# Order of the loads and of the score tiles around batch 1's attention, in a fused forgetting attention and GELU MLP

## The chip, the cores and the metric

The kernel runs on one core of one Trainium2 chip. A core has five engines that run at the same time, each through its own queue of instructions in order: TensorE (PE, matrix products; its weight loads are listed as PEld), VectorE (DVE), ScalarE (ACT, which has the exp and the GELU), GpSimd (POOL) and SyncE (SP, which only issues DMAs). Sixteen DMA engines move data between HBM and SBUF; their work comes from queues, and here the loads that POOL issues go through queue 0 and those that SP issues through queue 1. Matmuls write to PSUM, which has eight banks per partition. The metric is the device time of one execution in microseconds; the trace of one profiled execution says where it went.

## What is computed

```python
def _attn_ref(q, k, v, f):                  # q, k, v: (8, 8, 576, 64)   f: (8, 8, 576)
    scores = np.matmul(q, k.transpose(0, 1, 3, 2)) / np.sqrt(D)
    cum = np.cumsum(np.log(np.clip(f, 0.0001, 1.0)), axis=-1)
    decay = cum[:, :, :, None] - cum[:, :, None, :]
    scores = np.where(causal, -1000000000.0, scores + decay)
    attn = softmax(scores)                  # written out in the source
    return np.matmul(attn, v)

def _moe_ref(x, w_in, w_out):               # (4608, 512), (512, 2048), (2048, 512)
    h = x @ w_in
    g = 0.5 * h * (1.0 + erf(h / sqrt(2)))
    return g @ w_out

x = attn_out.transpose(0, 2, 1, 3).reshape(B * S, H * D)
```

There are 8 batches of 8 heads, 576 tokens and 64 features, then an MLP over the 4608 rows that the attention gives.

## The kernel before

**Tiles.** A batch is worked through in four pairs of heads (i = 0 to 3). For a pair, q and k have to stand transposed in `qT[i]` and `kT[i]`, features on the partitions, the two heads in the two halves. The causal triangle of scores of a pair is cut into four tiles (t = 0 to 3, `STILES` at L30): each is computed by PE into one of two score buffers of two PSUM banks (`scores`, L299), turned into `e` by one exp on ACT (L309), and, where it crosses the diagonal, masked. Batch 0 and pair 0 of batch 1 are masked by extra matmuls on PE; all others by POOL (L311), five instructions for a pair: two on tile 0, one on each of the others. Both score buffers are taken in turn, so a tile's matmuls wait until the exp of the tile two before it is done.

**v.** The forget gate enters as weights on v: `weigh_v(b, i)` multiplies the two heads of pair i by their weights (L268) and writes the weights in an extra column (L275). It runs on POOL for batch 1 and later. `attend` (L330) then multiplies e by the weighed v, 15 matmuls for a head, into one of two PSUM banks of the pool `o_psum`; `normalize` on DVE divides by the sums (L343, L344) and writes x. x is transposed into `xT`, by PE and a copy in batches 0 and 1 (`to_xT`, L363 and L366), by a DMA in the later ones (`x_dma`, L369).

**The MLP.** `gemm1` (L385) multiplies xT of a batch by w_in, one block of 128 features at a time, and ACT takes the GELU (L405). The second GEMM is spread as filler among the next attention's score tiles, through generators that `take(fill, n)` moves on by n matmuls. For batch 1 the filler is the first half of batch 0's rows, `gemm2_half(0, 0)` at L517: two PSUM banks, 16 matmuls, the first eight with the first quarter of w_out, the others with the second quarter. Batches 2 and later have longer fillers (L479).

**The order** is written out by hand: the context is `manual_schedule`, and each engine runs its instructions as the program lists them. `first_attention` holds batch 0, `second_attention` batch 1, `attention(b)` the rest. Between attentions the main loop at L727 runs the remaining blocks of `gemm1` and hangs preparation for the next batch on some of them.

**Loads.** POOL issues q, k, w_in and w_out (with a cast to bf16, L107, L171, L175). Each issue occupies POOL for 0.7 to 0.8 us. SP issues v in five pieces for the five blocks of 128 keys (`load_v`, L119, into the single buffer `v_sb`), the transposing DMAs of q and k of batch 2 and later (`transpose_dma`, L235) and of x, and the stores (L497). A queue of instructions is in order: an instruction that waits holds what is behind it. There is a small device for ordering a load behind something else: a one-column instruction on POOL that reads or writes a tile, so that what follows has to wait. The `memset` of a column of `v_sb` is one (the load of v that follows writes there, so it waits for POOL), `gate` another.

In batch 0's attention POOL issues, in this order, w_in's four quarters, q and k of batch 1 in two halves of four heads; SP issues v of batch 1 in two halves, one after the other. POOL then weighs pair 0 of batch 1 (program place: block 12 of the main loop for batch 0), issues w_out's quarters 0 and 1, weighs pair 1, and issues q and k of batch 2. The third and fourth quarters of w_out follow after the last score tile of batch 1. In `second_attention` each score tile is followed by something else: transposes of the next pair's q and k in pair 0, two filler matmuls in pairs 2 and 3, one head of the pair before after tiles 1 and 2.

`transposes_first` transposes q or k of a pair on PE (L207), six blocks of each head: first those of one head, then those of the other; the two heads go to the two halves of the PSUM partitions.

Of the kernel before, what the change touches and what calls it, by code (L numbers as in the profile page):

```python
# [8 lines left out]
FP32 = mybir.dt.float32  # L9
# [5 lines left out]
P = 128  # L15
S = 576
D = 64
H = 8
HP = 4
# [4 lines left out]
JT = 6  # L24
PT = 96
# [27 lines left out]
def kernel(  # L53
# [60 lines left out]
    def load_v(b, h0=0, h1=H):  # L114
        if b >= B:
            return
        for n in range(NBLK):
            p0 = D if n == NBLK - 1 else 0
            nc.sync.dma_start(  # L119
                v_sb[p0:P, h0:h1, n, :],  # L120
                v[b, h0:h1, K0[n] + p0 : K0[n] + P].rearrange("h p d -> p h d"),
            )
# [78 lines left out]
    def transposes_first(b, i, which, pool, tag):  # L201

        src = qk_of[b][which]
        ps = pool.tile([P, JT, PT], BF16, tag=tag, name="ps_f")
        for h in range(2):
            for j in range(JT):
                nc.tensor.transpose(  # L207
                    ps[h * D : (h + 1) * D, j, :],
                    src[:, 2 * i + h, j * D : (j + 1) * D],
                    ident_bf[:PT, :PT],  # L210
                )

        dst = (qT, kT)[which][i].rearrange("d (p j) -> d p j", j=JT)
        src = ps.rearrange("d j p -> d p j")
        if b or i:
            nc.vector.tensor_copy(dst, src)
        elif which:
            nc.vector.tensor_copy(dst[:, 0 : PT // 2], src[:, 0 : PT // 2])
            nc.scalar.copy(dst[:, PT // 2 :], src[:, PT // 2 :])
        else:  # L220
            nc.scalar.copy(dst, src)
# [315 lines left out]
    def take(gen, n):  # L537
        for _ in range(n):
            if next(gen, "end") == "end":
                return  # L540


    def gate(h, n):

        t = x_pool.tile([P, 1], FP32, tag="gate", name="gate")
        nc.gpsimd.tensor_copy(t[D:P], v_sb[D:P, h, n, 0:1])

    def first_attention():


# [44 lines left out]
        load_w_in(2)  # L595
        nc.gpsimd.memset(v_sb[:, :, 0, 0:1], 0.0)
        load_v(1, 0, 4)
        load_v(1, 4, 8)
        load_w_in(3)
        load_qk_tokens(1, 0, 4)  # L600
        load_qk_tokens(1, 4, 8)
        scores(0, 2, 1)
        heads = [(i, h) for i in range(3) for h in range(2)]
        for i, t in ((2, 2), (2, 3), (3, 0), (3, 1), (3, 2), (3, 3)):
# [28 lines left out]

    FILL = [[7, 6, 3, 3], [1, 3, 3, 2], [1, 3, 3, 3], [1, 3, 3, 3], [5]]
    FILL_2 = [[8, 8, 8, 8], [8, 8, 4, 4], [4, 4, 4, 4], [4, 4, 4, 4], [4]]
    FILL_1 = [[0, 0, 0, 0], [0, 0, 0, 0], [2, 2, 2, 2], [2, 2, 2, 2]]

    def attention(b):

# [9 lines left out]
        for i in range(HP):  # L649
            for t in range(4):  # L650
                scores(b, i, t)
                take(fill, counts[i][t])
                if i and t == 1:
                    av(i - 1)
                    x_dma(b, i - 1)
                if b == 2 and (i, t) == (0, 3):
                    weigh_v(b, 2)
                    weigh_v(b, 3)
                if i == 0 and t == (3 if b == 2 else 1):
                    load_v(b + 1)  # L660
                if b > 2 and t == 0 and i < 2:
                    transpose_dma(b + 1, 4 * i, 4 * i + 4)
                if b == 2 and t == 1 and i == 1:
                    transpose_dma(3, 0, 4)
# [21 lines left out]
    def second_attention():  # L686


        b, fill = 1, gemm2_half(0, 0)

        def av(i, h):
            attend(b, i, h, (0, 1, 2, 3, 4))
            normalize(b, i, h)

        def transposes(i, pool, tag):
            for which in range(2):
                transposes_first(b, i, which, pool, tag)


        nc.scalar.activation(warm[0:1, 0:1], warm[0:1, 0:1], Act.Exp)  # L700
        for i in range(HP):
            for t in range(4):
                scores(b, i, t)
                if i == 0 and t < 3:
                    transposes(t + 1, *((m_psum, "m") if t == 1 else (o_psum, "o")))
                take(fill, FILL_1[i][t])
                if i and t in (1, 2):
                    av(i - 1, t - 1)
                if i > 1 and t == 0:
                    to_xT(b, i - 2, nc.vector.tensor_copy, o_psum, "o")  # L710
                if i == 1 and t % 2:
                    weigh_v(1, 2 + t // 2)
                if (i, t) == (3, 3):
                    load_w_out(2)
                    load_w_out(3)
                if (i, t) == (3, 0):
                    transpose_dma(2, 0, 4)
                    transpose_dma(2, 4, 8)
        to_xT(b, HP - 2, nc.vector.tensor_copy, o_psum, "o")
        av(HP - 1, 0)  # L720
        av(HP - 1, 1)
        both = s_psum.tile([P, 2, 1024], BF16, tag="s", name="ps_x2")
        gemm1_begin(1, both)
        x_tail(1)
        load_v(2)

    for b in range(B):  # L727
# [8 lines left out]
        for ffb in range(4 if b < 2 else 5, n_ff):  # L736
            gemm1(b, ffb, ps=spare() if b > 1 and ffb in (7, 8) else None)
            if b == 0:
                if ffb == 14:
                    for which in range(2):  # L740
                        transposes_first(1, 0, which, o_psum, "o")
                if ffb == 12:
                    weigh_v(1, 0)
                    load_w_out(0)
                    load_w_out(1)
                    weigh_v(1, 1)
                    load_qk_tokens(2)
# [43 lines left out]
```

## Time and profile before

| | us |
|---|---|
| five runs | 342.55, 342.9, 343.3, 343.54, 343.72 |
| their median | 343.3 |
| the profiled execution, all of it | 344.4 |
| its span, from the first to the last instruction of the program | 342.3 |
| PE busy in the span | 327.4 |
| ACT / DVE / POOL busy | 209.7 / 185.1 / 121.7 |
| attention of batch 0, to the first GEMM | 0 to about 25 |
| first GEMM of batch 0 | 25 to 39.16 |
| attention of batch 1 | 39.16 to 60.45 |
| first GEMM of batch 1 | 60.45 to 73.59 |
| attention of batch 2 | 73.59 to 105.64 |

A span is counted from the first to the last instruction; the time of an execution has about 2 us around it. "Busy" is the time in which an engine runs at least one instruction. Matmuls are pipelined, so their listed durations overlap. In a timeline, a row gives the start, the busy time, the engine, the line, the operation, output and input tiles, the shape and, in brackets, how long the engine was idle before it and what ended that. In the chain of waits each row is the start, the length and the piece of work that was waited for. In the rows of the DMA queues the numbers are packets, MB, and the time that the packets took as a share of the sixteen engines.

The stretch that the change rewrites ends 60 us into the program; after it the same 280 us of GEMMs and attentions follow.

### The profile page before, as it was taken

How to read it: one execution, taken by the hardware profiler on the slowest of the kernel's cores; microseconds unless marked ns; L12 is line 12 of the kernel's file. 1: busy time of each engine (PE TensorE's matmuls, PEld its weight loads, DVE VectorE, ACT ScalarE, POOL GpSimd, SP SyncE). 2: the span in 40 equal slices, each digit the busy share in tenths (PEclk: the TensorE clock that was granted, in tenths of full speed). 3: DMA queues.
4: the chain of work that ended last, by engine and by line, in shares of the span. 5: the costliest groups of instructions: out<-in, count | busy, mean ns of one | idle time of the engine just before them, and what ended most of it. 6: DMA issues, size and time to landing. Idle time of an engine off the chain costs nothing.

```text
span 342.3 us, 7789 instructions
## 1 busy us (share of the span) xinstructions
PE 327.4 (96%) x3130; PEld 172.9 (51%) x3170; DVE 185.1 (54%) x418; ACT 209.7 (61%) x298; POOL 121.7 (36%) x247
## 2 busy tenths in 40 slices
PE   8799979999999999999999999999999999999995
PEld 4574545444554456545644465445544554444443
DVE  4770445662556944796469646984597541020011
ACT  6976777584553687378737873787468755504600
POOL 8190196009346134533445242724351420000000
PEclk9999999999999999999999999999999999999999
DMA  8999989997998989496977698589910242011013
GB/s 118 177 146 188 193 135 186 160 184 146 213 191 193 138 160 206 116 137 87 209 184 108 110 212 159 92 139 194 186 38 2 61 93 50 0 62 63 0 37 86
DMA packets 104627, 44.16 MB, mean 129 GB/s; under 512 B 83408, under 2 KB 100048, under 8 KB 104592
## 3 DMA queue, kind: packets, MB, share of 16 engines
q1 hardware_dynamic: 87296, 29.52, 44.5%
q0 software_dynamic: 16896, 13.63, 26.9%
q8 instruction: 24, 0.39, 0.5%
q10 hardware_dynamic: 400, 0.52, 0.4%
q14 instruction: 11, 0.09, 0.1%
HBM read 36.85 MB, written 9.44 MB: 135 GB/s over the span
## 4 chain that ended last, share of the span: by engine, by line
PE 82%; SPq 6%; DMA 4%; POOL 3%; issue 2%; DVE 1%; ACT 0%; POOLq 0%; DVEq 0%; ACTq 0%
PE ps L385 32%; PE ps L479 26%; PE o L330 8%; PE ps L421 8%; SPq L119 6%; PE s L299 6%; PE ps L517 2%; DMA v_sb<-in_v_dram 2%; DMA w_out_sb<-in_moe_w_out_dram 2%; POOL vw L268 1%; POOL q L107 1%; POOL k L107 0%; DVE vw L268 0%; DVE x L344 0%; PE ps_x L363 0%
## 5 line engine op out<-in xcount | busy, mean ns | idle before, releaser
L405 ACT ACTIVATE g<-ps 128x512 bf16<-128x512 f32 x144 | 82.1, 602 | 81.8 <-PE ps L385 81.8
L309 ACT ACTIVATE e<-s 128x896 bf16<-128x896 f32 (+2 forms) x128 | 101.4, 835 | 30.1 <-PE s L299 26.9
L385 PE MATMUL ps<-xT,w_in_sb 128*128 128x512 bf16 x502 | 111.7, 379 | 0.5
L479 PE MATMUL ps<-w_out_sb,g 64*128 64x512 bf16 (+1 forms) x712 | 102.1, 376 | 0.9 <-issue 0.5
L385 PEld LDWEIGHTS <-w_in_sb 128*128 128x128 bf16 x576 | 56.0, 98 | 67.5 <-issue 1.8
L311 POOL TENSOR_SCALAR_AFFINE_SELECT e<-e 128x256 bf16<-128x256 bf16 (+1 forms) x135 | 49.1, 383 | 94.9 <-ACT e L309 94.6
L479 PEld LDWEIGHTS <-g 64*128 64x128 bf16 (+1 forms) x736 | 41.9, 94 | 40.2 <-issue 9.3
L268 POOL TENSOR_TENSOR vw<-v_sb,wT 128x640 bf16<-128x640 f32 x30 | 38.6, 1289 | 38.3 <-DMA v_sb<-in_v_dram 30.0
L299 PE MATMUL s<-qT,kT 64*128 64x320 bf16 (+4 forms) x384 | 45.9, 277 | 2.8 <-ACT e L309 2.4
L249 DVE COPY kT<-tk 64x288 bf16<-64x288 bf16 x96 | 42.7, 445 | 3.3 <-DMA tk<-k 1.8
L249 DVE COPY qT<-tq 64x288 bf16<-64x288 bf16 x96 | 40.3, 420 | 3.0 <-DMA tq<-q 1.6
L330 PE MATMUL o<-vw,e 128*128 128x65 bf16 x960 | 37.1, 194 | 3.6 <-issue 2.4
L487 DVE COPY ot<-ps 128x512 f32<-128x512 f32 x25 | 17.3, 692 | 41.8 <-PE ps L479 41.8
L330 PEld LDWEIGHTS <-e 128*128 128x128 bf16 x960 | 34.5, 98 | 8.2 <-POOL e L311 2.8
L344 DVE TENSOR_TENSOR x<-o,r 128x320 bf16<-128x320 f32 x64 | 31.5, 492 | 2.2
L430 DVE COPY ot<-ps 128x512 f32<-128x512 f32 (+2 forms) x9 | 5.7, 633 | 48.8 <-PE ps L421 46.1
L299 PEld LDWEIGHTS <-kT 64*128 64x128 bf16 x384 | 19.3, 94 | 22.7 <-issue 9.4
L421 PE MATMUL ps<-w_out_sb,g 128*128 128x512 bf16 (+2 forms) x142 | 27.9, 355 | 0.1
L343 DVE RECIPROCAL r<-o 128x5 f32<-128x5 f32 x64 | 12.2, 190 | 22.5 <-PE o L330 22.5
L421 PEld LDWEIGHTS <-g 128*128 128x128 bf16 x144 | 13.5, 98 | 14.5
L490 DVE TENSOR_TENSOR ot<-ot,ps 128x512 f32<-128x512 f32 x25 | 17.2, 688 | 1.7 <-PE o L330 0.5
L385 PE MATMUL ps<-tails,w_in_sb 128*128 128x512 bf16 x62 | 14.2, 378 | 0.2
(64 smaller groups left out, 137.9 us busy)
## 6 DMA issues: line engine op xcount, KB each, us to landing
out_dram<-ot SPq DMA_DIRECT2D x32, 256.0 KB, 2.6
v_sb<-in_v_dram SPq DMA_DIRECT2D x24, 256.0 KB, 5.0
q<-in_q_dram POOLq DMA_DIRECT2D x6, 576.0 KB, 6.3
k<-in_k_dram POOLq DMA_DIRECT2D x6, 576.0 KB, 8.4
v_sb<-in_v_dram SPq DMA_DIRECT2D x22, 128.0 KB, 5.8
w_in_sb<-in_moe_w_in_dram POOLq DMA_DIRECT2D x4, 512.0 KB, 8.0
w_out_sb<-in_moe_w_out_dram POOLq DMA_DIRECT2D x4, 512.0 KB, 8.0
q<-in_q_dram POOLq DMA_DIRECT2D x4, 144.0 KB, 4.7
```

What stands on the lines that cost most here:

```text
L119: nc.sync.dma_start(v_sb[p0:P, h0:h1, n, :], v[b, h0:h1, K0[n] + p0 : K0[n] + P].rearrange("h p d -> p h d"),)
L249: nc.vector.tensor_copy(rows[:, odd], src[odd * D : (odd + 1) * D, 2 * i + h].rearrange("d j p -> d p j"),)
L268: eng.tensor_tensor(vw(b)[:, hs, :, 0:D], v_sb[:, hs, :, :], w.unsqueeze(3).to_broadcast([P, 2, NBLK, D]), Alu.mult,)
L299: nc.tensor.matmul(to, *ab, start=half < 0, stop=half == 1 or not masked)
L309: nc.scalar.activation(et[:, :, z:c], st[:, :, z:c], Act.Exp, scale=scale)
L311: nc.gpsimd.affine_select(out=et[:, :, c0 + z : c0 + P], in_=et[:, :, c0 + z : c0 + P], compare_op=Alu.is_ge, fill=0.0, base=z, pattern=[[ ...
L330: nc.tensor.matmul(o[:, m, :], e_of[b, i, t][:, h, c : c + P], vw_of[b][:, 2 * i + h, n, :], start=(n == 0), stop=(n == m),)
L344: nc.vector.tensor_tensor(x_of[b, i][:, :, h, :], o[:, :, 0:D], r.unsqueeze(2).to_broadcast([P, NBLK, D]), Alu.mult,)
L385: nc.tensor.matmul(ps, w_in_sb[:, kt, ffb * P : (ffb + 1) * P], src[:, kt, 0:TC], start=(kt == 0), stop=(kt == n_dm - 1),)
L405: nc.scalar.activation(g_of[c][ffb], ps, Act.Gelu)
L421: nc.tensor.matmul(pss[ts][:, c0:c1], g_of[c][kt][:, ts * P : (ts + 1) * P], w_out_sb[:, kt, c0:c1], start=(kt == 0), stop=(kt == n_ff - 1),)
L479: nc.tensor.matmul(banks[r], g_of[c][kt][rows, ts * P : (ts + 1) * P], w_out_sb[rows, kt, :], start=kt == (steps.index("r") if r else 0), ...
```

## The change

Four things change.

- In `first_attention`, `load_v(1, 4, 8)` is taken out and `load_w_out(0)` is put behind the loads of q and k of batch 1. At block 12 of the main loop for batch 0, `behind(qk_of[1][0], H - 1)` makes POOL wait until q's second half has landed, a `memset` of `v_sb`'s heads 4 to 7 makes SP wait for that, and `load_v(1, 4, 8)` follows; `load_w_out(0)` is no longer there.
- `second_attention` is written out anew: score tiles come two at a time (`tiles`), the transposes of pairs 1 and 2 stand behind the first two tiles and those of pair 3 behind the next two, both heads of a pair are attended together (`run`), the 16 filler matmuls come in four groups of four, and the transposes of x of pairs 0, 1 and 2 come later than before. The transposes of x of pair 2 go to a score buffer, and their copy to ACT in place of DVE. A second `behind` makes POOL wait for k of batch 2 before it issues w_out's third and fourth quarters.
- In `attention(2)`, `load_v(3)` is moved from behind tile 3 of pair 0 to behind the transposing DMA of x of pair 0.
- `transposes_first` alternates between the two heads instead of doing one after the other, in batches 0 and 1.

```diff
--- before.py
+++ after.py
@@ -202,8 +202,8 @@
-        for h in range(2):
-            for j in range(JT):
+        for j in range(JT):
+            for h in range(2):
                 nc.tensor.transpose(
                     ps[h * D : (h + 1) * D, j, :],
                     src[:, 2 * i + h, j * D : (j + 1) * D],
@@ -545,6 +545,11 @@
+    def behind(t, h):
+
+        g = x_pool.tile([P, 1], FP32, tag="gate", name="gate")
+        nc.gpsimd.tensor_copy(g[:PT], t[:, h, 0:1])
+
     def first_attention():
@@ -595,10 +600,10 @@
         load_w_in(2)
         nc.gpsimd.memset(v_sb[:, :, 0, 0:1], 0.0)
         load_v(1, 0, 4)
-        load_v(1, 4, 8)
         load_w_in(3)
         load_qk_tokens(1, 0, 4)
         load_qk_tokens(1, 4, 8)
+        load_w_out(0)
         scores(0, 2, 1)
@@ -633,7 +638,6 @@
-    FILL_1 = [[0, 0, 0, 0], [0, 0, 0, 0], [2, 2, 2, 2], [2, 2, 2, 2]]
@@ -653,10 +657,12 @@
                 if i and t == 1:
                     av(i - 1)
                     x_dma(b, i - 1)
+                    if b == 2 and i == 1:
+                        load_v(3)
                 if b == 2 and (i, t) == (0, 3):
                     weigh_v(b, 2)
                     weigh_v(b, 3)
-                if i == 0 and t == (3 if b == 2 else 1):
+                if b > 2 and i == 0 and t == 1:
                     load_v(b + 1)
@@ -698,28 +704,45 @@
-        for i in range(HP):
-            for t in range(4):
-                scores(b, i, t)
-                if i == 0 and t < 3:
-                    transposes(t + 1, *((m_psum, "m") if t == 1 else (o_psum, "o")))
-                take(fill, FILL_1[i][t])
-                if i and t in (1, 2):
-                    av(i - 1, t - 1)
-                if i > 1 and t == 0:
-                    to_xT(b, i - 2, nc.vector.tensor_copy, o_psum, "o")
-                if i == 1 and t % 2:
-                    weigh_v(1, 2 + t // 2)
-                if (i, t) == (3, 3):
-                    load_w_out(2)
-                    load_w_out(3)
-                if (i, t) == (3, 0):
-                    transpose_dma(2, 0, 4)
-                    transpose_dma(2, 4, 8)
-        to_xT(b, HP - 2, nc.vector.tensor_copy, o_psum, "o")
-        av(HP - 1, 0)
-        av(HP - 1, 1)
+        def tiles(i, t):
+            scores(b, i, t)
+            scores(b, i, t + 1)
+
+        def run(i):
+            av(i, 0)
+            av(i, 1)
+
+        tiles(0, 0)
+        transposes(1, o_psum, "o")
+        transposes(2, m_psum, "m")
+        tiles(0, 2)
+        transposes(3, m_psum, "m")
+        tiles(1, 0)
+        run(0)
+        tiles(1, 2)
+        take(fill, 4)
+        weigh_v(1, 2)
+        tiles(2, 0)
+        run(1)
+        weigh_v(1, 3)
+        tiles(2, 2)
+        take(fill, 4)
+        tiles(3, 0)
+        transpose_dma(2, 0, 4)
+        transpose_dma(2, 4, 8)
+        take(fill, 4)
+        to_xT(b, 0, nc.vector.tensor_copy, o_psum, "o")
+        tiles(3, 2)
+        behind(qk_of[2][1], H - 1)
+        load_w_out(2)
+        load_w_out(3)
+        run(2)
+        to_xT(b, 1, nc.vector.tensor_copy, o_psum, "o")
+        take(fill, 4)
+        av(3, 0)
         both = s_psum.tile([P, 2, 1024], BF16, tag="s", name="ps_x2")
+        to_xT(b, 2, nc.scalar.copy, ps=both[:, 0, 0:XC])
+        av(3, 1)
         gemm1_begin(1, both)
         x_tail(1)
         load_v(2)
@@ -740,8 +763,10 @@
                 if ffb == 12:
+                    behind(qk_of[1][0], H - 1)
+                    nc.gpsimd.memset(v_sb[:, 4:8, 0, 0:1], 0.0)
+                    load_v(1, 4, 8)
                     weigh_v(1, 0)
-                    load_w_out(0)
                     load_w_out(1)
                     weigh_v(1, 1)
                     load_qk_tokens(2)
```

## The prediction

> **What bounds the kernel now.** I read the busy shares first, then the stretch that the change rewrites (batch 1's attention) by windows, then the chain of waits through it, then POOL's and the DMA queues' part of that chain.
>
> ```profile
> PE 327.4 (96%) x3130; PEld 172.9 (51%) x3170; DVE 185.1 (54%) x418; ACT 209.7 (61%) x298; POOL 121.7 (36%) x247
> ```
>
> TensorE (PE) is busy for 96% of the span, so a change gains only where PE stands idle. Batch 1's attention runs from 39.16 us, when batch 0's first GEMM has been issued, to 60.45, where the last x of batch 1 is transposed and batch 1's first GEMM streams.
>
> ```profile
> 39.16:44.50 5.34, 4.23 (x106) 3.33 (x107) 4.22 (x7) 5.13 (x8) 3.20 (x5) 1.00 0.66 134
> 44.50:49.45 4.95, 3.16 (x48) 2.03 (x49) 1.46 (x5) 3.81 (x5) 4.95 (x9) 1.00 0.99 154
> 49.45:57.46 8.01, 7.93 (x100) 4.36 (x99) 4.33 (x11) 5.54 (x7) 5.44 (x15) 1.00 1.30 200
> 57.46:60.45 2.99, 2.68 (x43) 1.88 (x45) 1.77 (x5) 2.00 (x3) 1.92 (x3) 1.00 1.10 153
> 60.45:73.59 13.14, 13.09 (x62) 5.74 (x60) 9.19 (x28) 8.63 (x15) 0.42 (x1) 1.00 1.18 184
> ```
>
> The columns after the stretch and its length are busy us of PE, weight load, DVE, ACT, POOL, then clock, DMA share, GB/s. PE idles 1.1 us in the first stretch and 1.8 in the second, where POOL is busy throughout; from 49.45 it is packed, and after 60.45 too. The clock is full, so none of this is throttling. What the second stretch waits for stands in the chain:
>
> ```profile
> 37.22 4.02 DMA v_sb<-in_v_dram
> 41.30 1.27 POOL vw L268
> 42.67 5.94 DMA w_out_sb<-in_moe_w_out_dram
> 48.65 0.38 PE ps L517
> 57.77 0.41 POOL e L311
> 60.16 0.45 PE ps_x L363 x5
> ```
>
> The first quarter of w_out is issued by POOL only after POOL has waited for v and weighed a pair; it lands 5.94 us later, and PE, which has the matmul at L517 next, starts it at 48.65 after 1.44 us of waiting. Batch 1's remaining score tiles stand behind it, so ACT starves too. At the end a mask of POOL (57.77) decides.
>
> **The change, part by part.** *w_out(0) earlier.* It joins POOL's queue behind batch 1's q and k, and is in SBUF some 4 us earlier, so the 1.44 us go. What is late next is POOL:
>
> ```profile
> 41.30 1.27 POOL L268 TENSOR_TENSOR vw<-v_sb,wT 128x640 bf16<-128x640 f32 x1 [14.98 <-DMA v_sb<-in_v_dram]
> 42.67 1.56 POOL L175 DMA_DIRECT2D w_out_sb<-in_moe_w_out_dram  x2
> 45.60 0.84 POOL L107 DMA_DIRECT2D q<-in_q_dram  x1
> 47.20 1.02 POOL L311 TENSOR_SCALAR_AFFINE_SELECT e<-e 128x256 bf16<-128x256 bf16 x3
> ```
>
> Let W be the start of the first weighing. POOL then has that weighing with its small copy, 1.37 (41.30 to 42.67); one w_out issue, 0.78 (half of 1.56); the second weighing, 1.37; q and k of batch 2, 1.60 (45.60 to 47.20); and pair 1's five masks, 1.71 (three from 47.20 to 48.18, two from 49.55 to 50.29). Pair 1 is masked at W+6.83. W cannot come before 41.3, since v's first half keeps its place in its queue; it can come up to 1 us later, because w_out's packets now take engines that v had alone near the end (below). I take 41.6, near the first bound, as the slowest engines were still carrying k then. Masks done: 48.45.
>
> PE's new order needs that mask in head (1,0): ten of its 15 matmuls and head (1,1) follow, 0.8 us by the row at 58.23 (25 matmuls in 0.97): 49.3. Then two score tiles 0.55; four L517 matmuls, 0.86 (eight took 1.73); tile (3,0); a wait of 0.3, as tile (3,1) needs the exp of (2,3) to free its buffer, and exps run at 0.6 to 0.8 each; 51.7. Four L517, 0.86; transposes of x(0), 0.35; tiles (3,2), (3,3) 0.6, to 53.5. Pair 2's two heads 1.0, to 54.5. Transposes of x(1) need the PSUM bank of head (2,0), free when DVE's reciprocal and multiply end (0.39 to start, 0.2 + 0.5): a wait of 0.6, to 55.1, and 0.3 of work. Four L517 to 56.3; head (3,0) 0.55; transposes of x(2) 0.4; head (3,1) 0.5 and drain: 58.0. In the trace of before, 1.25 us lie between that point (58.23 + 0.97 = 59.20) and 60.45. So 59.25 in place of 60.45: **1.2 us earlier**. ACT is covered: its sixteen exps need 11.6 us from 41.2 (five took 3.62), and the last mask, after exp (3,3) at about 54.9, is done by 55.4, before head (3,0) at 56.3 asks. Without that cover each us of lateness costs one.
>
> *Half of v later.* Heads 4 to 7 of batch 1 are issued once POOL has seen q land (23.76 + 15.2 = 38.96): about 39.2. They are 4x128 + 64 KB in 256 B packets, 2304 of them.
>
> ```profile
> q0 software_dynamic: 2087, 1.75, 91.3%
> q1 hardware_dynamic: 2034, 0.51, 32.1%
> ...
> q1 hardware_dynamic: 993, 0.25, 112.7%
> q0 software_dynamic: 28, 0.02, 11.1%
> ```
>
> The first two lines are 26 to 38 us: beside a full queue 0 (POOL's) v gets one packet for one, 170 per us. The last two are 40 to 41 us: alone it gets 993 per us. w_out(0) is 512 packets of 1 KB; with queue 0 at 667 in 4 us (22 to 26 us) it ends near 43. Queue 0 is then empty until w_out(1), issued at W+1.37 = 43.0, sends its first packet, about 1.9 us later (in the trace of before none has moved by 44, issued at 42.67). So v has the engines alone for nearly 2 us, 1900 packets, and a rest of up to 400 at 170 per us. It lands between 45.5 and 49. Call it L. Pair 2's heads come at L + 1.37 + 0.98 + 1.37 + 0.73 = L + 4.45 (two weighings, four steps of masks; POOL is in order, so masks of pair 2 queue behind the weighing that waits). They are due at 53.5: L up to 49.05 is free, and from 50.25 on the change loses.
>
> The Trainium skill, "DMA: Bandwidth & Descriptors", section Specifications, gives about 0.6 us to the first byte for a DMA issued by SP. This trace differs: of v issued at 21.81, 32 packets had moved by 26, against 667 of queue 0. By the page v would start at 39.8 and land early in my interval, by the row late in it; the sum is 342.1 by either.
>
> *w_out(1), batch 2's q and k.* Their issues on POOL are counted above. w_out(1) is asked for by the third group of L517 at 51.7 and lands by 43.0 + 5.94 = 48.9; cover 2.8 us. k of batch 2 follows about 3 us earlier than its 57.8 (46.42 + 11.4), as one w_out quarter less stands ahead of it. The gate on k ahead of w_out(2), (3) therefore opens near POOL's last mask, and the transposes and v of batch 2, which hang on k in SP's queue, move forward as much or more than PE. Cost 0; were k no earlier, w_out(2) would land at 65.4 as now (58.12 + 7.3), still ahead of 72.7, when the first matmul of batch 2's fill reads it (73.89 - 1.2).
>
> *Transposes with heads alternating.* In the trace 24 of them take
>
> ```profile
> 39.91 0.47 PE L207 MATMUL ps_f<-key_of,q 96*64 96x96 bf16 x10
> ...
> 40.66 0.20 PE L299 MATMUL s<-qT,kT 64*128 64x64 bf16 x2
> ```
>
> 0.75 us, 31 ns each. Gain between 0 and 0.1 us per group, off the path: the groups of batch 0 end in the wait for v, those of batch 1 in ACT's table load, which ends at 41.1. The Trainium skill, "TensorEngine Tiling (Array Packing)", section Theoretical Speedup, promises up to 2x for 64 columns, which would be 0.37 per group; the rows around 40.2, where q's and k's transposes start in turns, show that most of the overlap is there already. The price is 0 by both, as the groups lie under other waits.
>
> *x of batch 2 ahead of v(3).* SP issues the transposing DMA of x (93.90 in the trace) before v's five, which take 7.67 us of SP from 85.38. x is 6 us earlier, nobody waits for it before 105.6; v lands perhaps 2 us later than its 95.8 (90.46 + 5.3), read at 101.47 by a POOL instruction that then waits for PE anyway. Price 0, with 0.5 either way if these covers are thinner than they look.
>
> **Sum.** The profiled execution has a span of 342.3 us, 344.4 in all; 2.1 lie around the span. 342.3 - 1.2 = 341.1. The five runs have a median of 343.3, 1.1 below the profiled one, so I put the gain on the median: **342.1 us**. The likeliest case's own range is 340.6 (W at 41.3, neither wait of PE: 2.4 gained, and 0.3 of the spread of the runs) to 343.0.
>
> **Rivals.** (a) *The wait only moves to POOL, nothing is left:* with W at 42.6, as w_out's packets hold up the end of v's first half, every step above shifts by 1 us and 59.25 becomes 60.25: 343.1. For it: POOL is busy for all of the second stretch. Against it: the slowest engines had no free time to lose. (b) *v's second half comes late:* if queue 0 never runs dry, L = 40.7 + 2304/170 = 54.3, pair 2 starts at 58.75 in place of 53.5, and GEMM at 64.5: 4 us lost, 347.3; it loses from L = 50.25. For it: the one-for-one share over 12 us. Against it: POOL cannot issue w_out(1) before it has weighed a pair. (c) *Given back later:* the GEMM starts 1.2 us earlier but batch 2's loads do not; PE then waits at 71 to 85 and the time is 343.3. Against it: k and v of batch 2 move with it.
>
> **How the numbers follow.** Of a difference under 0.2% (0.7 us) a measurement of this kernel cannot tell. The forecast has 0.60; (a) and (c) 0.17 together; (b) 0.23, most of it with L between 51 and 54, 344 to 347. Faster 0.60, same 0.17, slower 0.23. The range that leaves out 2 in 10 reaches from 340.5 to 345.0.
>
> **What would show it.** Right: no wait for w_out at L517; POOL's first weighing at 41.3 to 42; the weighing of pair 2 at POOL without a wait for v, or one ending by 49; GEMM streaming at 59.25, and the same 281.9 us from there to the end. Wrong: POOL waiting for v past 50; PE waiting on a mask or on DVE between 49 and 56 for more than 0.9 us in all; a first weighing after 42.5; or new idle time of PE after 60.

## The result and the profile after

Side by side the changed kernel takes 341.7 us (median of 54 runs, 340.61 to 347.39) and the kernel before 343.71 (94 runs, 342.15 to 347.54). The ratio is 0.9948, with a 95% interval of 0.9936 to 0.9959: 1.4 to 2.2 us faster. The forecast was 342.1. In 12 of the 54 executions the mean granted clock of PE was below 0.998, and these have a median of 344.15; the other 42 have 341.3. The profiled execution took 341.23, with a span of 339.2.

The busy shares of the changed kernel, from its page:

```profile
PE 325.6 (96%) x3129; PEld 171.6 (51%) x3170; DVE 184.4 (54%) x417; ACT 209.9 (62%) x299; POOL 121.8 (36%) x250
```

No engine has less work to speak of (PE's 1.8 us are within what such a total moves: two traces of the kernel before have 327.4 and 331.8, the first with 40 matmul records fewer). What changed is how long the stretch of batch 1's attention takes. Its windows, with the same columns as before (stretch and length, busy us of PE, weight load, DVE, ACT, POOL, then clock, DMA share, GB/s):

```profile
38.50:43.50 5.00, 3.84 (x110) 3.00 (x110) 3.55 (x6) 4.91 (x8) 3.90 (x6) 1.00 1.13 208
43.50:48.50 5.00, 4.75 (x80) 2.99 (x79) 2.69 (x8) 4.46 (x6) 4.28 (x8) 1.00 1.23 191
48.50:54.35 5.85, 5.26 (x63) 3.08 (x64) 2.93 (x8) 4.65 (x7) 5.29 (x16) 1.00 1.23 182
54.35:57.35 3.00, 2.95 (x47) 2.01 (x46) 1.72 (x5) 2.11 (x3) 1.51 (x2) 1.00 1.19 101
57.35:70.50 13.15, 13.04 (x62) 5.79 (x62) 10.26 (x32) 9.08 (x16) 0.42 (x1) 1.00 1.21 203
```

In what follows "the section" runs from the first score tile of batch 1 (39.45 before, 38.50 after) to the GEMM behind the last transposes of x (60.45 and 57.35). It falls from 21.01 to 18.86 us. After it come 281.89 us before and 281.85 after, the same. The remaining 0.95 us of the difference between these two spans lies ahead of the section; a second trace of the kernel before has its first tile at 38.94, so part of that is the spread from execution to execution.

The clearest view of the section is ScalarE's timeline (start, busy time, operation, tiles, shape of the first, count; in brackets the idle time before the row and what ended it). The kernel before:

```profile
41.21 2.40 ACT L309 ACTIVATE e<-s 128x896 bf16<-128x896 f32 x3
43.77 3.62 ACT L309 ACTIVATE e<-s 128x640 bf16<-128x640 f32 x5 [0.16 <-PE s L299]
47.62 0.92 ACT L309 ACTIVATE e<-s 128x896 bf16<-128x896 f32 x1 [0.23 <-ACT e L309]
49.89 0.81 ACT L309 ACTIVATE e<-s 128x768 bf16<-128x768 f32 x1 [1.36 <-PE s L299]
...
56.99 0.70 ACT L309 ACTIVATE e<-s 128x640 bf16<-128x640 f32 x1 [0.34 <-PE s L299]
```

The changed kernel:

```profile
40.26 4.68 ACT L309 ACTIVATE e<-s 128x896 bf16<-128x896 f32 x6
45.10 1.51 ACT L309 ACTIVATE e<-s 128x896 bf16<-128x896 f32 x2 [0.17 <-PE s L299]
46.98 3.03 ACT L309 ACTIVATE e<-s 128x896 bf16<-128x896 f32 x4 [0.37 <-ACT e L309]
50.33 3.24 ACT L309 ACTIVATE e<-s 128x896 bf16<-128x896 f32 x4 [0.32 <-PE s L299]
```

Sixteen exps, one for each score tile. Before, they stretch over 16.49 us (41.21 to 57.70), with 3.77 us of gaps, the largest (1.36) where PE stood at L517 for w_out and could not feed ACT. After, they are packed into 13.31 us (40.26 to 53.57) with 1.02 us of gaps. So each section is a sum of three pieces: 1.76 us from the first score tile to the first exp, the stretch of exps, and a tail from the last exp to the GEMM.

| | first exp | stretch of exps | tail | section |
|---|---|---|---|---|
| before | 1.76 | 16.49 | 2.75 | 21.01 |
| changed | 1.76 | 13.31 | 3.78 | 18.86 |

The exps gain 3.18 us, and the tail gives 1.03 back: the new order leaves pair 2's heads, a group of filler and two groups of x transposes behind the last score tile. The difference is 2.15 us.

POOL's timeline in the changed kernel answers to the rows shown of before:

```profile
39.59 1.27 POOL L268 TENSOR_TENSOR vw<-v_sb,wT 128x640 bf16<-128x640 f32 x1 [1.49 <-DMA v_sb<-in_v_dram]
...
40.95 0.81 POOL L175 DMA_DIRECT2D w_out_sb<-in_moe_w_out_dram  x1
...
43.98 0.78 POOL L107 DMA_DIRECT2D k<-in_k_dram  x1
44.76 1.01 POOL L311 TENSOR_SCALAR_AFFINE_SELECT e<-e 128x256 bf16<-128x256 bf16 x3
46.09 0.41 POOL L311 TENSOR_SCALAR_AFFINE_SELECT e<-e 128x256 bf16<-128x256 bf16 x1 [0.31 <-ACT e L309]
46.68 0.41 POOL L311 TENSOR_SCALAR_AFFINE_SELECT e<-e 128x256 bf16<-128x256 bf16 x1 [0.19 <-ACT e L309]
47.30 1.28 POOL L268 TENSOR_TENSOR vw<-v_sb,wT 128x640 bf16<-128x640 f32 x1 [0.22 <-POOL e L311]
...
54.06 0.18 POOL L551 CAST gate<-k 96x1 f32<-96x1 bf16 x1
```

The first weighing starts at 39.59; pair 1 is masked at 47.09 (46.68 + 0.41); the last two of these masks wait for ACT, not ACT for them. The weighing of pair 2 follows 0.2 us later. And PE's timeline, the three rows on which the prediction had put a number:

```profile
45.23 1.04 PE L517 MATMUL ps<-w_out_sb,g 128*128 128x512 bf16 x3
...
48.65 0.31 PE L299 MATMUL s<-qT,kT 64*128 64x320 bf16 x2 [0.25 <-ACT e L309]
...
53.71 0.45 PE L363 MATMUL ps_x<-key_of,x 128*128 128x128 bf16 x5 [0.34 <-DVE x L344]
```

The filler at L517 has no bracket: it waits for nothing. The two waits that remain are of 0.25 and 0.34 us.

### The profile page after: what moved, and what is told of

It reads as the page before. It is cut to its first block, busy times and chain, and to the rows that moved or that the text cites. A ratio compares the mean times of both kernels' runs of the same rounds, so it can differ in the third digit from the quotient of the medians.

```text
span 339.2 us, 7794 instructions
## 1 busy us (share of the span) xinstructions
PE 325.6 (96%) x3129; PEld 171.6 (51%) x3170; DVE 184.4 (54%) x417; ACT 209.9 (62%) x299; POOL 121.8 (36%) x250
## 4 chain that ended last, share of the span: by engine, by line
PE 88%; DMA 3%; issue 3%; ACT 2%; POOL 1%; DVE 1%; SPq 0%; POOLq 0%; ACTq 0%
PE ps L385 36%; PE ps L479 25%; PE o L330 9%; PE ps L421 8%; PE s L299 7%; DMA v_sb<-in_v_dram 2%; ACT e L309 2%; PE ps L517 2%; DMA xT<-x 1%; PE ps_x L363 1%; POOL q L107 1%; SPq L119 0%; POOL k L107 0%; PE ps_f L207 0%; DVE x L344 0%
## 5 line engine op out<-in xcount | busy, mean ns | idle before, releaser
L268 POOL TENSOR_TENSOR vw<-v_sb,wT 128x640 bf16<-128x640 f32 x30 | 38.6, 1288 | 23.9 <-DMA v_sb<-in_v_dram 15.3
L249 DVE COPY kT<-tk 64x288 bf16<-64x288 bf16 x96 | 43.9, 457 | 2.0 <-DMA tk<-k 0.5
L249 DVE COPY qT<-tq 64x288 bf16<-64x288 bf16 x96 | 39.1, 407 | 3.1 <-DMA tq<-q 1.7
```

Of the source, the lines that this page charges most:

```text
L249: nc.vector.tensor_copy(rows[:, odd], src[odd * D : (odd + 1) * D, 2 * i + h].rearrange("d j p -> d p j"),)
L268: eng.tensor_tensor(vw(b)[:, hs, :, 0:D], v_sb[:, hs, :, :], w.unsqueeze(3).to_broadcast([P, 2, NBLK, D]), Alu.mult,)
```

## The experiments

Every kernel was timed side by side with the kernel before. "Ratio" is to that, with its 95% interval. "At full clock" is the median of those executions whose mean granted clock was 0.998 or more, and their number; for the kernel before it was 343.4 to 343.5 in each of the three groups of runs that these kernels stand beside. That split was made afterwards and leaves few runs, so it is weaker evidence than the ratio. The last columns are from the one profiled execution of each.

| kernel | median, us (runs) | ratio | at full clock, us (runs) | exps | tail | section | after it |
|---|---|---|---|---|---|---|---|
| loads only | 343.87 (12) | 1.0024 [0.9992, 1.0057] | 342.97 (7) | 16.81 | 2.75 | 21.33 | 281.98 |
| order only | 343.36 (12) | 0.999 [0.9966, 1.0015] | 342.92 (7) | 15.56 | 3.80 | 21.11 | 281.63 |
| alternation only | 343.05 (12) | 0.9991 [0.9963, 1.0018] | 342.81 (8) | 16.03 | 2.76 | 20.54 | 281.87 |
| w_out(0) early only | 343.39 (12) | 0.9988 [0.9962, 1.0015] | 342.98 (11) | 14.95 | 2.75 | 19.46 | 281.86 |
| the same, masks first | 342.5 (12) | 0.9965 [0.9944, 0.9987] | 342.5 (12) | 14.95 | 2.75 | 19.46 | 281.85 |
| v's half later still | 350.53 (4) | 1.0179 [1.0138, 1.0221] | none | 13.31 | 12.57 | 27.64 | 281.62 |
| v's half early | 342.02 (12) | 0.9952 [0.9923, 0.998] | 341.73 (9) | 13.31 | 3.77 | 18.85 | 281.63 |
| v(3) ahead of x | 342.5 (12) | 0.996 [0.9937, 0.9982] | 341.57 (9) | 15.03 | 3.57 | 20.35 | 282.14 |
| no gate on k | 341.59 (8) | 0.9945 [0.9919, 0.9971] | 341.52 (7) | 13.32 | 4.18 | 19.25 | 281.62 |
| two weighings on DVE | 341.6 (12) | 0.9946 [0.9915, 0.9976] | 340.73 (7) | 13.31 | 3.35 | 18.43 | 281.60 |
| changed, again | 341.46 (12) | 0.9947 [0.9918, 0.9975] | 341.21 (7) | 13.31 | 3.80 | 18.87 | 281.61 |
| before, again | 343.59 (12) | 0.9997 [0.997, 1.0023] | 343.59 (12) | 16.85 | 2.75 | 21.36 | 281.95 |

**The loads alone.** To the kernel before, the moves of the loads in batch 0 and nothing else.

```diff
-        load_v(1, 4, 8)
...
+        load_w_out(0)
...
                 if ffb == 12:
+                    behind(qk_of[1][0], H - 1)
+                    nc.gpsimd.memset(v_sb[:, 4:8, 0, 0:1], 0.0)
+                    load_v(1, 4, 8)
                     weigh_v(1, 0)
-                    load_w_out(0)
```

> Before with the loads of the change alone (w_out's first quarter behind q and k of batch 1, v's second half behind q), old order of the score tiles. Theory 1, loads and order need each other: PE's wait of 1.44 us for w_out at L517 goes, POOL's masks come 0.8 us earlier, and head (1,0) then waits for the mask behind the weighing of pair 2; the distance from the first score tile of batch 1 to its first GEMM after the last x (21.0 us in the trace of before, 18.85 in that of after) falls to 20.0 to 20.5, the time by 0.5 to 1.0 us. Theory 2, the loads are all of it: 18.9 and 1.8 us. Theory 3, the order is all of it: 21.0 and no change.

No gain that the runs can tell: ratio 1.0024, section 21.33. (Five of the twelve executions, at 346.2 to 346.4, had a clock of 0.995; the other seven lie 0.5 us below the kernel before, and the profiled one is the slowest of those seven.) The wait at L517 is gone, and another has taken its place. POOL's timeline and, below it, ScalarE's:

```profile
45.20 1.02 POOL L311 TENSOR_SCALAR_AFFINE_SELECT e<-e 128x256 bf16<-128x256 bf16 x3
47.85 1.28 POOL L268 TENSOR_TENSOR vw<-v_sb,wT 128x640 bf16<-128x640 f32 x1 [1.63 <-DMA v_sb<-in_v_dram]
...
49.23 0.76 POOL L311 TENSOR_SCALAR_AFFINE_SELECT e<-e 128x256 bf16<-128x256 bf16 x2
```

```profile
50.93 0.92 ACT L309 ACTIVATE e<-s 128x896 bf16<-128x896 f32 x1 [2.32 <-PE s L299]
```

In the old order the weighing of pair 2 stands between the third and the fourth mask of pair 1. With v's second half landing at 47.69, POOL waits 1.63 us with masks queued behind it; PE waits for the masks, and ACT idles 2.32 us in place of 1.36.

**The order alone.** The new `second_attention` (with its gate on k), the alternating transposes and the place of v(3), on the old loads.

```diff
+        load_v(1, 4, 8)
...
-        load_w_out(0)
...
                 if ffb == 12:
-                    behind(qk_of[1][0], H - 1)
-                    nc.gpsimd.memset(v_sb[:, 4:8, 0, 0:1], 0.0)
-                    load_v(1, 4, 8)
                     weigh_v(1, 0)
+                    load_w_out(0)
```

(This diff is against the changed kernel.)

> After with the old loads (w_out's first quarter issued by POOL after the first weighing, v's halves one after the other). Theory 1: the first group of four filler matmuls is due about 1 to 2.5 us before w_out lands, and PE waits there with all score tiles of pairs 2 and 3 behind it; the distance is 20.5 to 22, the time between 0.5 us faster and 1 us slower than before. Theory 2, loads are all: 21.0, no change. Theory 3, the order is all: 18.9, 1.8 us faster.

No gain that the runs can tell: 0.999, section 21.11. The chain of waits (start, length, piece of work) still goes through w_out:

```profile
41.95 5.86 DMA w_out_sb<-in_moe_w_out_dram
47.80 0.05 issue
47.85 0.39 PE ps L517
```

ACT then idles 2.63 us ahead of its ninth exp. Neither half of the change gives anything by itself that the ratio can tell; together they give 1.8 us. At full clock the loads and the order are each 0.5 us below the kernel before, and together 2.1: the whole is about twice the sum of its halves.

**Alternation alone.**

```diff
-        for h in range(2):
-            for j in range(JT):
+        for j in range(JT):
+            for h in range(2):
```

> Before with the alternating transposes alone. My prediction: 24 transposes take 0.65 in place of 0.75 us, and nothing of it is seen in the time (0 to 0.1 us). Rival: the trace of after starts batch 1's score tiles at 38.5 in place of 39.45, and if the alternation is what shortens batch 0's attention, this run is 0.9 us faster. If it is neither, v of batch 0 landed earlier by chance in the profiled run, and the landing time of v's first half (13.9 to 15.9 us) differs from trace to trace with the start of the score tiles following it.

The 24 transposes of a pair do get shorter (0.53 us from the first to the first of the next 24 in the changed kernel, where 0.75 stood before; the prediction had at most 0.1 us of gain for a group, and it was 0.22), but the ratio is 0.9991, from 1.3 us gained to 0.6 lost. Its section of 20.54 is 0.5 to 0.8 below the two traces of before, and at full clock its runs are 0.6 below: the runs neither bear out a gain of that size nor exclude it, so the price of 0 is not shown.

**What of the order is needed.** The kernel before with w_out's first quarter early and v untouched; then the same with the weighings of pairs 2 and 3 behind the masks.

```diff
+        load_w_out(0)
...
-                    load_w_out(0)
...
-                if i == 1 and t % 2:
-                    weigh_v(1, 2 + t // 2)
+                if (i, t) in ((1, 3), (2, 1)):
+                    weigh_v(1, i + 1)
```

The first run has only the lines on `load_w_out(0)`, the second all of them.

> The kernel before with one edit: the first quarter of w_out is issued behind q and k of batch 1; both halves of v keep their old place. Theory A (the order on POOL eats the gain): the wait at L517 goes, but v's second half lands at 46 to 47.5 us, the weighing of pair 2 stands ahead of the last masks of pair 1 in POOL's queue, and the section from the first score tile of batch 1 to the next GEMM stays at 20.2 to 21.3 us (before: 21.0); time 0 to 0.6 us below before. Rival B (only the wait for w_out mattered; v's late half in the runs so far spoilt it): with both halves of v early the weighing finds v in place, the section falls to 19.6 us or less, and the time by 1.2 us or more.

> As the run before it, and with the weighings of pairs 2 and 3 behind the masks of pair 1 and the first masks of pair 2 in POOL's queue; the score tiles keep their old order. Theory A (the order on POOL ate the gain of the loads): the masks of pair 1 are done by 48.5 us, the section shrinks to 19.3 to 20 us, and the time is 1.0 to 1.7 us below before. Rival C (the order of the score tiles on PE and ACT is what is needed, not POOL's): the section stays above 20.3 us and the time within 0.6 us of before.

With the weighings still ahead of the masks the ratio is 0.9988; with the masks first it is 0.9965, 1.2 us below before (0.4 to 1.9), and the section 19.46. POOL's timeline of the second kernel:

```profile
46.46 0.41 POOL L311 TENSOR_SCALAR_AFFINE_SELECT e<-e 128x256 bf16<-128x256 bf16 x1 [0.50 <-ACT e L309]
47.06 0.41 POOL L311 TENSOR_SCALAR_AFFINE_SELECT e<-e 128x256 bf16<-128x256 bf16 x1 [0.19 <-ACT e L309]
47.43 1.28 POOL L268 TENSOR_TENSOR vw<-v_sb,wT 128x640 bf16<-128x640 f32 x1
```

Pair 1 is masked by 47.47 with the score tiles in the old order, so the rival that PE's order of tiles is what was needed falls: swapping two places in POOL's queue and one load is worth about two thirds of the whole by the ratios (1.0 of 2.1 us at full clock). What remains goes with the rest of the change; in the traces it is the new order of tiles (exps 14.95 to 13.31, tail 2.75 to 3.78). That the swap by itself is worth 0.9 us (0.5 at full clock) is less sure: the intervals of the two kernels overlap, and the trace of the first can't decide. In it the first score tile stands at 41.98 (the clock, below), so its loads had 3 us more, v's second half landed at 45.26, ahead of the weighing at 48.87, and its section of 19.46 is better than its median shows. The intended contrast between theory A and rival B was lost in that trace; the medians lean to A.

**v's second half later, and early.** Both on the changed kernel. Later: its issue behind that of w_out's second quarter. Early: right behind the first half, without gate.

```diff
-                    behind(qk_of[1][0], H - 1)
-                    nc.gpsimd.memset(v_sb[:, 4:8, 0, 0:1], 0.0)
-                    load_v(1, 4, 8)
                     weigh_v(1, 0)
                     load_w_out(1)
+                    nc.gpsimd.memset(v_sb[:, 4:8, 0, 0:1], 0.0)
+                    load_v(1, 4, 8)
```

(Early: the same three lines go, and `load_v(1, 4, 8)` follows `load_v(1, 0, 4)` in batch 0.)

> After with v's second half issued behind w_out's second quarter in place of behind q of batch 1, some 3 us later, into a time in which POOL's queue is full. Rival (b) of the prediction: v shares one packet for one, lands 10 to 13 us after its issue, at 53 to 57; pair 2's heads start 4.45 us after the landing and the GEMM 9.5 to 10.2 us after it, at 63 to 67: 4 to 7 us slower than before, 347 to 351. If late v were covered by the new order, the time stays near 342.

> After with v's second half issued directly behind the first half, as before; w_out's first quarter stays early. If what counts is only that w_out is early and v's second half in time, this equals after within 0.5 us: w_out lands before 45.5 and v before 47. Rival: putting v's second half behind q is what lets v's first half land early (W 1.1 us after the first score tile in after, 1.7 to 1.8 in the two traces with the old loads); then W comes 0.5 to 1 us later and the time is up to 1 us longer than after.

Later costs 9.1 us against the changed kernel timed beside it (350.53 against 341.46). POOL's timeline and, below it, PE's:

```profile
46.81 0.41 POOL L311 TENSOR_SCALAR_AFFINE_SELECT e<-e 128x256 bf16<-128x256 bf16 x1 [0.19 <-ACT e L309]
54.65 1.28 POOL L268 TENSOR_TENSOR vw<-v_sb,wT 128x640 bf16<-128x640 f32 x1 [7.43 <-DMA v_sb<-in_v_dram]
```

```profile
58.83 1.92 PE L330 MATMUL o<-vw,e 128*128 128x65 bf16 x28 [2.06 <-POOL e L311]
...
66.27 2.10 PE L385 MATMUL ps<-xT,w_in_sb 128*128 128x512 bf16 x9
```

v lands at 54.13, pair 2's heads run from 58.83 (4.70 us later) and the GEMM behind the last transposes of x starts at 66.27, 12.14 us after the landing and not 9.5 to 10.2; the stretch of exps is as short as ever, and everything is lost in the tail. Early makes no difference that the runs can tell: 0.9952. (Its median is 0.6 us above the changed kernel's, within what the rival gave and less than such a measurement resolves. In its trace the first tile stands at 41.61, so its loads had 3 us more and its section of 18.85 can't decide.) So no gain of the later issue of v's second half is shown; it is only cheap enough as long as v still lands by about 48.

**The moves with price 0.** v(3) back at its old place in batch 2 (ahead of x); and POOL's wait for k of batch 2 taken out.

```diff
-                    if b == 2 and i == 1:
-                        load_v(3)
...
-                if b > 2 and i == 0 and t == 1:
+                if i == 0 and t == (3 if b == 2 else 1):
```

```diff
-        behind(qk_of[2][1], H - 1)
```

> After with v of batch 3 issued ahead of x of batch 2 again, as before. My prediction: no change to after (within 0.5 us), since nobody waits for either. Rival: the move gives some of the 1.8 us; then this run is slower than after by it and PE has new idle time between 70 and 105 us.

> The changed kernel without the wait of POOL for k of batch 2 ahead of w_out's third and fourth quarters. Theory (the gate opens at 54.06 us, just as POOL ends its last mask at 54.04, so it holds nothing): the time is that of the changed kernel within 0.4 us, the GEMM starts 18.9 us after the first score tile as before, and as many us follow it (281.6 to 282.1). Rival (the gate keeps w_out's packets away from k and so buys part of the gain): k lands 1 us or more later and the time rises by 0.5 us or more.

The first has 0.996, with an interval that holds the changed kernel's 0.9948, and 282.14 us behind the section, where the changed kernel's two traces have 281.85 and 281.61: 0.3 to 0.5 us, none of it sure. Its section is long for another reason, seen on POOL:

```profile
42.59 1.28 POOL L268 TENSOR_TENSOR vw<-v_sb,wT 128x640 bf16<-128x640 f32 x1 [2.69 <-DMA v_sb<-in_v_dram]
...
47.76 1.73 POOL L311 TENSOR_SCALAR_AFFINE_SELECT e<-e 128x256 bf16<-128x256 bf16 x5
```

In this one execution v's first half landed only at 42.43, although nothing that runs before it differs from the changed kernel. Pair 1 is then masked at 49.49, and the section is 20.35.

The second has 0.9945 and 281.62 us behind the section: the time is the same without the gate. k of batch 2 did land 1.3 us later than in the changed kernel (55.31), as the rival had it, but the time did not rise. That the gate holds nothing is true of the changed kernel's trace; in that of the v(3) kernel it held POOL for 1.34 us. That the section was 19.25 and not 18.9 is a miss; POOL's timeline shows v's second half late by 1.16 us, not the gate:

```profile
48.52 1.28 POOL L268 TENSOR_TENSOR vw<-v_sb,wT 128x640 bf16<-128x640 f32 x1 [1.16 <-DMA v_sb<-in_v_dram]
...
52.25 2.44 POOL L311 TENSOR_SCALAR_AFFINE_SELECT e<-e 128x256 bf16<-128x256 bf16 x7
54.64 1.57 POOL L175 DMA_DIRECT2D w_out_sb<-in_moe_w_out_dram  x2
```

**What bounds the section now.** Two of POOL's weighings given to DVE, and a group of filler put ahead of the transposes of x(1).

```diff
         transposes(3, m_psum, "m")
+        weigh_v(1, 1, nc.vector)
...
-        weigh_v(1, 3)
+        weigh_v(1, 3, nc.vector)
...
-        to_xT(b, 1, nc.vector.tensor_copy, o_psum, "o")
         take(fill, 4)
+        to_xT(b, 1, nc.vector.tensor_copy, o_psum, "o")
...
-                    weigh_v(1, 1)
```

> After with pairs 1 and 3 of batch 1 weighed by DVE in place of POOL, and the fourth group of filler matmuls ahead of the transposes of x of pair 1 (PE waits 0.34 us for DVE there in the trace of after). If POOL decides whenever W is late, pair 1 is masked at W + 5.5 in place of W + 6.9, a late W costs 1.4 us less, and the median falls by 0.3 to 1.0 us below after. If ACT decides in most runs, only the 0.3 us come, within the noise.

The exps take 13.31 us again, to the hundredth, so they did not wait for POOL in either execution. But v's first half was in place before the first tile in this one, which stands at 42.02, so what the weighings on DVE do for a late W isn't shown. The tail is 0.43 us shorter, and at full clock the runs are 0.5 below the changed kernel's (340.73 against 341.21, seven each), which fits. The ratio, 0.9946, can't be told from the 0.9947 of the changed kernel beside it: whether it is a better version is open.

**Repeats.**

> The changed kernel once more, for a second trace of it and to stand beside the others on this chip. In four traces of kernels with its loads or its order, POOL's first weighing of batch 1 (W) starts 1.1 to 3.4 us after the first score tile of batch 1. If POOL's queue decides, as predicted (pair 1 masked at W + 6.83), the first GEMM after the last x lies at W + 17 in a trace with a late W, and at the first score tile + 18.9, where ACT's exps decide, in one with an early W. Time 341 to 342.5, ratio to before 0.993 to 0.997.

> The kernel before, once more, for a second trace of it. If the difference ahead of the first score tile (39.45 us before, 38.50 in the changed kernel) is chance, this trace has the first tile at 38.5 to 39.5, a section of 20.6 to 21.3 us, and a ratio within 0.2% of 1. If it belongs to the change, the first tile stands at 39.4 or later again.

The changed kernel gave 0.9947 and a section of 18.87, the kernel before 0.9997 and 21.36. Of the 0.95 us ahead of the section, the second trace of before leaves 0.3 (38.94 against 38.64).

## Why the prediction was right, and where it was off

- *The forecast, 342.1 by a section 1.2 us shorter.* Right in its mechanism, with the gain a third too small. That the time was only 0.4 us off is in part luck: the kernel before came out at 343.71, not at the 343.3 that the forecast started from, so the gain was 1.8 us (1.4 to 2.2) and not 1.2. The GEMM streams at 57.35, not 59.25: 0.95 us of that lies ahead of the section, 0.95 in it. The section shrank by 2.15 us in the traces, the time by 1.8 in the runs' ratio. The clock fits the difference: over both groups of runs of the changed kernel, the 49 of 66 executions at full clock have a median of 341.26, 2.1 below the 343.40 of the kernel before (99 of 107, timed with the experiments); the other 17, against 8 of before, have 344.31. Whether the change itself makes such executions more frequent isn't shown: they are 5 of 12 with the loads alone, 5 with the order alone, 4 with the alternation, none with w_out's quarter early and the masks first. The trace of the v(3) kernel shows another loss: with a late first half of v the section gains 0.7 only.
- *W, the start of POOL's first weighing: the term that was mis-sized.* "W cannot come before 41.3" tied it to one trace's clock time. In the changed kernel it was 39.59 and 39.71, 1.1 us behind the first score tile where the prediction had 2.15; its own sign of being right, a first weighing at 41.3 to 42, did not come. With 1.09 in place of 2.15 the prediction's section is 18.74 us, against 18.86. That this fits so closely is chance: from W to the GEMM the sum has 17.65 us, and 16.95 were measured where POOL decides (the v(3) kernel); in the changed kernel it was 17.76, where the masks waited for ACT. v's first half landed 0.92 and 0.90 us after the first tile, against 1.68 and 2.04 in the two traces of before. Why it comes earlier isn't settled: w_out's packets were expected to hold it up. Of the seven traces with w_out first and full clock ahead of the section it landed 0.37 to 1.08 us after the first tile in six and 3.24 in one; in the four with w_out later, 1.19 to 2.04.
- *Pair 1 masked at W + 6.83.* Shown where POOL decides: 49.49 - 42.59 = 6.90 in the v(3) kernel. In the changed kernel it was W + 7.50, because with an early W the masks wait for the exps. So the prediction's statement that ACT is covered was wrong by the time W came early: ACT's 12.29 us of exps (13.31 less 1.02 of gaps; the prediction had 11.6, though its own trace has 12.72) set the section from there.
- *PE's waits of 0.3 and 0.6.* The second was right in place, 0.34 in size. The first, 0.25, stood at tile (2,3) and not at (3,1): ACT was already behind two tiles earlier than the prediction had it.
- *No wait at L517, w_out(1) in time.* Right: it landed at 46.87 and was asked for at 50.34.
- *L between 45.5 and 49, free up to 49.05.* L was right: 47.04. The bound was too generous: without the gate on k v landed at 48.35, and the tail was already 0.4 us longer, since PE asks for pair 2's heads at 52.24 and not at 53.5. The rows of the DMA queues in the changed kernel (packets, MB, share of sixteen engines), 38 to 40 us and 40 to 43 us, show the gap that the prediction counted on:

```profile
q0 software_dynamic: 419, 0.40, 121.9%
q1 hardware_dynamic: 33, 0.01, 3.1%
...
q1 hardware_dynamic: 1896, 0.47, 73.1%
q0 software_dynamic: 164, 0.15, 34.5%
```

  v, issued at 38.13, moves 33 packets until 40 and 1896 in the next three microseconds, when queue 0 has next to nothing. The Trainium skill's 0.6 us to a first byte ("DMA: Bandwidth & Descriptors", Specifications) is not what these rows show as a flow: that takes some 2 us.
- *The GEMM at L + 10.2 when v decides (64.5 less 54.3, in rival (b)).* Tested with v late: L + 12.14. POOL's part held (heads of pair 2 at L + 4.70, predicted L + 4.45); the rest lies behind them, at half the clock, below.
- *Rival (a), POOL late:* this is what happens in single executions (W at 42.59, section 20.35), not in the typical one. *Rival (b), v late:* its mechanism is real, and it was priced too low: with v at 54.13, where the rival had 54.3, the time was 350.53 and not 347.3. The place in the change avoids it. *Rival (c), given back later:* false, 281.85 us against 281.89; k of batch 2 landed at 54.01 in place of 57.78, and the gate opened at 54.06, right behind the last mask (53.63 + 0.41).
- *What the prediction did not say* is that the load and the order need each other. It wrote "the 1.44 us go" of w_out and found POOL late next, which is right for the new order; in the old order the same load gains nothing by the ratio, and about 0.5 us by the runs at full clock.

## What to carry to other kernels

When a wait for a load stands on the critical path, look at what is queued next on the engine that released it: moving the load alone moved the wait to a mask behind a weighing in POOL's queue, and most of the gain came only when that queue was put in the order in which its results are asked for. Price a step relative to the event that starts its stretch, not to the clock time of one trace; landing times shift by microseconds from execution to execution. A load moved later with no gain to show for it is a liability that stays hidden until its cover runs out, and then each microsecond costs at least a full one.

## What the runs showed of the hardware

**PE's clock can halve after little idleness.** In three of the profiled executions (w_out early only, v's half early, weighings on DVE) the first score tile of batch 1 stands at 41.6 to 42.0 us in place of 38.5 to 39.5. Windows of the first of them, clock in the third column from the end:

```profile
12.00:14.00 2.00, 1.51 (x36) 1.10 (x32) 1.08 (x3) 2.00 (x3) 0.00 (x0) 1.00 1.21 237
14.00:16.00 2.00, 0.84 (x17) 0.67 (x16) 0.38 (x1) 0.98 (x2) 0.18 (x1) 0.83 0.48 103
16.00:22.00 6.00, 5.43 (x82) 4.18 (x81) 3.74 (x8) 3.24 (x4) 5.57 (x7) 0.50 0.89 153
22.00:24.00 2.00, 2.00 (x46) 1.47 (x42) 1.37 (x5) 1.52 (x2) 2.00 (x4) 0.97 1.18 187
```

PE waits 1.16 us for k of batch 0 from 14.06 on, and from 15.3 to 22.1 it has half its clock although it is busy; that costs some 3 us ahead of the section and nothing in it. In the changed kernel the longest wait of PE in that part of batch 0's attention was 0.51 us, and the clock stayed at 1.00. The kernel with v late shows the same inside the section:

```profile
52.00:54.00 2.00, 0.39 (x4) 0.09 (x1) 0.64 (x2) 1.59 (x3) 0.00 (x0) 1.00 1.32 201
54.00:56.00 2.00, 0.00 (x0) 0.00 (x0) 0.00 (x0) 0.00 (x0) 1.35 (x2) 0.64 1.37 138
56.00:64.00 8.00, 5.45 (x57) 3.88 (x58) 1.85 (x5) 0.58 (x1) 6.45 (x16) 0.50 0.85 137
```

PE stands still from 52.4, and its clock is halved from 54.55 until 64.79. From 58.83 to the GEMM it takes 7.44 us, where the changed kernel takes 5.11 from 52.24 for nearly the same work: its loss is larger than the lateness of v alone. The Trainium skill, "TensorE: Matmul & The Clock Gate", Part 1, has the clock halved after an idle window of about 3.4 us and restored after a busy one. The lengths agree: in the clock records of the four traces half clock lasts 6.83 us three times and 10.24 us once, which is twice and three times 3.41, and in the last 3.41 us of each PE was busy throughout. But the 3.41 us ahead of the halving were not idle: PE was busy for 2.08, 1.76, 1.45 and 1.26 us of them. The length of one wait does not decide either. In the kernel with v's half early no wait of PE in those 3.41 us was longer than 0.44 us, while a wait of 1.07 us at 15.79 in the trace of before and one of 1.38 us at 15.33 in that of the v(3) kernel left the clock at 1.00. What decides isn't shown. A halved clock makes such stalls dearer than the waits that the trace lists, and it hits some executions of a kernel and not others.

**Landing times are not fixed.** v's second half landed between 6.7 and 11.2 us after the one-column write that lets it be issued, in six executions of kernels that issue it at the same place (39.80 to 46.48 and 40.01 to 51.18 are the extremes). The 2.0 us that the changed kernel had to spare by the prediction's own bound (47.04 to 49.05), or the 1.3 us to the landing at 48.35 that already cost something, are thin beside that.
